# A Fourier layer and a soft mixture of experts on one core: the head's loads, warm-up matmuls and first units in another order

## The chip, the core and the metric

The kernel runs as one launch on one core of a Trainium2 chip. The metric is the device time of a run in microseconds (us), taken as the median over several runs. A core has five engines, each with its own queue that is worked strictly in order: TensorE (PE in the profile, with its weight loads as PEld), VectorE (DVE), ScalarE (ACT), GpSimd (POOL) and SyncE (SP). SP issues nearly all DMAs here, ACT the few that the head's first stores and, after the change, one load need.

## The reference, cut to what matters

```python
X = np.fft.rfft(x, axis=1)                       # x: 8 x 2496 x 256, float32
Yr = Xr @ w_r - Xi @ w_i + b_r
Yi = Xr @ w_i + Xi @ w_r + b_i
Y = softshrink(Yr, 0.01) + 1j * softshrink(Yi, 0.01)
y = np.fft.irfft(Y, n=2496, axis=1).reshape(19968, 256)
logits = y @ phi                                 # 32 slots: 8 experts x 4
d = softmax(logits over all 19968 tokens)        # dispatch
slot_out = per expert: relu(d.T @ y @ w1) @ w2
out = softmax(logits over the 32 slots) @ slot_out
```

## The kernel before, in words

The transform of length 2496 = 39 x 64 is done as two small ones. **Stage a** (`a_unit`, L326) multiplies 117 rows of x (three sets of 39) by the constant `f1a`, two columns of 64 at a time: a *unit*, 512 wide, whose result `pa` lies in PSUM. A batch has 11 units. ACT or DVE copies each `pa` into a staging tile `ast`, and `ast` is stored to DRAM (`adr`, or `ad0` for the first 48 rows of batch 0), because the second transform needs the data with other rows on the partitions. **Stage b** runs in steps of four of the 20 frequencies: `load_ap` (L384) reads a group back as `ap` in two DMAs, `f2` (L392) multiplies it by `smov` into `px` (two halves c = 0, 1), ACT and DVE split `px` into a high and a low part (`xth`, `xtl`) and do the same with the sum of its real and imaginary parts (`xsm`, split into `xsh`, `xsl`). `lin_k` (L445) and `lin_y` (L456) multiply these by the split weights into `pk` and `py`; DVE adds bias and shrinks (`ut`, `rt`, whose last subtraction is POOL's). Later stages project on phi (`pq`), transpose (`pt`), and run the inverse transform and the softmaxes on 32 slots for each batch, then the experts, then the output.

Batch 0 is special: its x comes as eleven loads (`x0`), all units are plain fp32 (`direct`: one matmul instruction in the program, which the profile shows as two), and its stores are cut in two. The rows that groups 0 and 1 need go to `ad0` by four stores on ACT's queue; the other 80 rows wait in the list `rest` and are stored by SP later. Batch 1 begins inside the head as well: its first four units are fp32 too (`nd` is 4), and their two staging tiles are kept in `held` until SP's list calls for their store. From the fifth unit on the rows are split into `xh` (ACT) and `xl` (POOL), and a unit is three matmuls.

The order of all engines is written by hand. Each piece of work is a generator that yields the time at which it wants to go on (in units of the plan, not in us); a heap (`run_until`) replays them in that order, and `keep_in_program_order` freezes it. The numbers of the dictionary `PLAN` (L118 on) are these wishes: `a1` for the units of batch 1, `kw` for the warm-up matmuls (`keep_warm`, products of a zero tile that nobody reads), `seq` for the order of SP's DMAs in the head (`a0` is `load_ap` of group 0, `r` the next of the four rest stores, `w4` and `w0` the held stores, `x8` a load of batch 1's x, `c` and `k` constants, `s` the second part of `smov`). Tiles come from pools with few buffers: `ap` has 3, `ast` 3, `wr` 3, `xr` 3; a tile that takes a used buffer waits for its last reader.

DMAs report on eight semaphores in turn (DMAHW0 to DMAHW7), in the order in which the program issues them, SP's and ACT's together. A DMA waits until the previous one on its semaphore has landed, so the ninth waits for the first.

Of the kernel before, what the change touches and what calls it, by code (L numbers as in the profile page):

```python
# [11 lines left out]
F32 = mybir.dt.float32  # L12
F32R = mybir.dt.float32r
AF = mybir.ActivationFunctionType
ALU = mybir.AluOpType
AX = mybir.AxisListType

B, N, D = 8, 2496, 256
# [32 lines left out]
def _constants():  # L51
# [95 lines left out]
    "f1": [1.5, 2.15],  # L147
    "kw": [[-40, 9]],
    "ap1": 1.85,
# [8 lines left out]
    "cl_": 'V',  # L158
    "a1": [-50, -49, -48, -47, 3.0, 4.0, 5.9, 6.9, 7.9, 8.9, 10.2],
    "e1": [0, 0, 0, 0, 0, 0, 0, 0, 1, 0, 1],  # L160
# [4 lines left out]
    "lsl": 'PPPPPPPPPPPPPPPPPPPPPPPV',  # L165
    "ast4": {(0, 18): "wr", (1, 0): "wr", (1, 4): "ap"},
    "nd": 4,
    "x1": {(1, 20): 3.5, (2, 0): 7.2},
    "ab1": [[0, 4], [4, 8], [8, 14], [14, 20], [20, 22]],
    "seq": ['a0', 'c', 'a1', 's', 'x8', 'r', 'r', 'r', 'r', 'w4', 'a2', 'x9', 'x10', 'w0', 'k'],  # L170
}
# [12 lines left out]
def fourier_soft_moe_kernel(ctx: ExitStack, tc: tile.TileContext, t: dict, out: bass.AP):  # L184
# [51 lines left out]
    def sp(**kw):  # L236
        tc.keep_in_program_order(nc.sync.dma_start(**kw))
# [16 lines left out]

    def load_x(i):
        if i >= len(xorder) or xorder[i] in xrs:
            return
        b, g = xorder[i]
        ng = min(xc, G - g)
        xr = wtile([PX, xc, D], F32, "xr", f"xr{b}_{g}")  # L260
        sp(out=xr[:, :ng, :], in_=x[b, :, g : g + ng, :])
        xrs[(b, g)] = xr
# [63 lines left out]
    def a_unit(b, g, u):  # L326
# [26 lines left out]
        ast = asts[(b, gs[0])]  # L353
        po = psum(("pf", "pl", "pt")[i_ % 3] if first else "pf", f"pa{b}_{g}")
        if direct:
            mm(out=po, lhsT=f1a, rhs=xs, start=True, stop=True)
        else:
            mm(out=po, lhsT=f1h, rhs=xh, start=True, stop=False)
            mm(out=po, lhsT=f1h, rhs=xl, start=False, stop=False)
            mm(out=po, lhsT=f1l, rhs=xh, start=False, stop=True)  # L360
        yield tu + PLAN['ao']
        copy(
# [4 lines left out]
        if g + GP == gs[1]:  # L367
            if b == 1 and direct:
                held[gs[0]] = (ad[b], ast, *gs)
                return  # L370
            yield tu + 1.0
            if first:
                a_write(ad0, ast, *gs, 0, R * 4 * KG, q=aq)
                rest.append((ad[b], ast, *gs, R * 4 * KG, QA))
            else:
                a_write(ad[b], ast, *gs)
# [7 lines left out]
    def load_ap(b, grp):  # L384
        ap = wtile([128, KG, D], F32, "ap", f"ap{b}_{grp}")
        src = (ad0 if b == 0 and grp < 2 else ad[b]).rearrange("(k r) g d -> k (r g) d", r=R)
        src = src[grp * 2 * KG : (grp + 1) * 2 * KG, :N2]
        for c in range(2):
            sp(out=ap[c::2], in_=src[c * KG : (c + 1) * KG].rearrange("k n d -> n k d"))
        return ap  # L390

    def f2(s, c, t0):  # L392
        yield t0
        b, grp = steps[s]
        ap = aps[s]
        ps = psum("pf", f"px{b}_{grp}_{c}")
        for j in range(KG):
            k = grp * KG + j
            q = k if grp == 0 else k - KG
            rhs = smov[min(grp, 1)][:, 0 : q + 2 : q + 1, :]  # L400
            mm(
                out=ps[:, j * 128 : (j + 1) * 128],
                lhsT=ap[:, j, c * 128 : (c + 1) * 128],
                rhs=rhs,
                start=True,
                stop=True,
            )
        yield t0 + PLAN['xho']
        xh = wtile([128, 2, KG, 64], F32R, "xth", f"xth{b}_{grp}_{c}")
        xl = wtile([128, 2, KG, 64], F32R, "xtl", f"xtl{b}_{grp}_{c}")  # L410
        pv = ps.rearrange("p (j c q) -> p c j q", j=KG, c=2)
        sm = wtile([128, KG, 64], F32, "xsm", f"xsm{b}_{grp}_{c}")
        sh = wtile([128, KG, 64], F32R, "xsh", f"xsh{b}_{grp}_{c}")
        sl = wtile([128, KG, 64], F32R, "xsl", f"xsl{b}_{grp}_{c}")
        A.copy(out=xh, in_=pv)
        A.copy(out=sm, in_=pv[:, 0])
        yield t0 + PLAN['xlo']
        V.tensor_tensor(out=xl, in0=pv, in1=xh.bitcast(F32), op=ALU.subtract)
        V.tensor_tensor(out=sm, in0=pv[:, 1], in1=sm, op=ALU.add)
        yield t0 + PLAN["sho"]  # L420
        copy(E_("sh"), sh, sm)
        yield t0 + PLAN["slo"]
        (L_("sl", s, c) if s else V).tensor_tensor(out=sl, in0=sm, in1=sh.bitcast(F32), op=ALU.subtract)
        xts[(s, c)] = (xh, xl, sh, sl)

# [19 lines left out]
    def lin_k(s):  # L445
        t0 = 4 * s
        yield t0 + 0.35
        b, g = steps[s]
        pk = psum("pl", f"pk{b}_{g}")
        for c in range(2):  # L450
            lin_s(pk, c, xts[(s, c)])
        yield t0 + PLAN['ko']
        kss[s] = wtile([128, 2, 256], F32, "k1", f"k1{b}_{g}")
        A.copy(out=kss[s], in_=pk.rearrange("p (e x) -> p e x", e=2))

    def lin_y(s, e):  # L456
        b, grp = steps[s]
        end = s == ns - 1
        t0 = 4 * s + 1 + (PLAN["T_"]["ye"] if end else 1.35) * e
        yield t0  # L460
        py = psum("pl", f"py{b}_{grp}_{e}")
        lin(py, e, 0, xts[(s, 0)])
        if e == 1 and not end:
            t0 = 4 * s + 3
            yield t0
# [300 lines left out]
    sp(out=wri, in_=t["w"])  # L766
    load_x(7)
    for u, g in enumerate(range(0, G, GP)):
# [494 lines left out]
```

## Time and profile before

| | us |
|---|---|
| median of 3 runs | 567.42 |
| lowest and highest of them | 566.44 and 567.63 |
| the profiled execution | 563.34 |
| its span, first to last instruction | 561.5 |
| PE busy in the span | 521.4 |
| first product of group 0 (`px`) starts at | 23.53 |
| first product of group 2 starts at | 39.68 |

The profile is of one execution. The timeline lists an engine's instructions in order of time: start, length, engine, line, operation, out<-in, count, and in brackets how long the engine had stood idle and what ended that. The windows view gives, for chosen stretches, each engine's busy time, the clock that the PE was granted (1.00 is full), the busy share of the 16 DMA engines and the rate of their traffic. The chain of waits is followed back from the end: at each step to what released the instruction. An engine's idle time matters only where that engine, or what it feeds, is what the rest waits for. All helpers record their instructions under one line (L243 for matmuls, L180 for the other engines, L237 and L240 for DMAs on SP and ACT), so the tiles' names tell the pieces apart.

### The profile page before, as it was taken

How to read it: one execution, taken by the hardware profiler on the slowest of the kernel's cores; microseconds unless marked ns; L12 is line 12 of the kernel's file. 1: busy time of each engine (PE TensorE's matmuls, PEld its weight loads, DVE VectorE, ACT ScalarE, POOL GpSimd, SP SyncE). 2: the span in 40 equal slices, each digit the busy share in tenths (PEclk: the TensorE clock that was granted, in tenths of full speed). 3: DMA queues.
4: the chain of work that ended last, by engine and by line, in shares of the span. 5: the costliest groups of instructions: out<-in, count | busy, mean ns of one | idle time of the engine just before them, and what ended most of it. 6: DMA issues, size and time to landing. Idle time of an engine off the chain costs nothing.

```text
span 561.5 us, 11780 instructions
## 1 busy us (share of the span) xinstructions
PE 521.4 (93%) x4354; PEld 442.2 (79%) x4354; DVE 422.0 (75%) x837; ACT 298.1 (53%) x650; POOL 281.1 (50%) x258
## 2 busy tenths in 40 slices
PE   8669999999999999999999999999899979899794
PEld 4458999989898889889988898987687867367573
DVE  0347897799979897989789978986795764248783
ACT  4435555666566656665665666653433333147572
POOL 0037777766766576658655866684554402000100
PEclk9999999999999999999999999999999998999899
DMA  8788464756476637664757474766634378979898
GB/s 301 249 294 292 151 207 152 210 179 170 163 216 207 189 118 208 207 180 167 204 171 199 155 201 167 222 230 178 186 131 126 113 183 276 392 240 368 325 374 351
DMA packets 93684, 121.44 MB, mean 216 GB/s; under 512 B 46786, under 2 KB 68736, under 8 KB 93628
## 3 DMA queue, kind: packets, MB, share of 16 engines
q1 hardware_dynamic: 93372, 119.63, 65.4%
q10 hardware_dynamic: 256, 1.08, 0.5%
q8 instruction: 34, 0.56, 0.4%
q14 instruction: 22, 0.18, 0.1%
HBM read 69.87 MB, written 50.82 MB: 215 GB/s over the span
## 4 chain that ended last, share of the span: by engine, by line
PE 70%; DVE 13%; DMA 10%; ACT 3%; issue 2%; SPq 1%; ACTq 0%; DVEq 0%
PE py L243 16%; PE px L243 11%; PE pq L243 9%; PE pa L243 8%; PE pk L243 7%; PE pt L532 4%; PE pr L243 3%; DMA eb<-ed 2%; PE pc L1067 2%; DMA ad<-ast 2%; PE pe L243 2%; DMA ap<-adr 2%; DVE mx L180 1%; DVE clpL L180 1%; DVE xtl L180 1%
## 5 line engine op out<-in xcount | busy, mean ns | idle before, releaser
L180 POOL TENSOR_TENSOR rt<-ut,rt 128x512 f32<-128x512 f32 x79 | 111.7, 1414 | 24.4 <-DVE rt L180 18.4
L180 POOL TENSOR_TENSOR xsl<-xsm,xsh 128x256 fp32r<-128x256 f32 x77 | 59.3, 770 | 102.4 <-DVE xsh L180 71.0
L180 POOL TENSOR_TENSOR xl<-xr,xh 117x512 fp32r<-117x512 f32 x73 | 98.5, 1350 | 22.6 <-ACT xh L180 14.7
L243 PE MATMUL px<-smov,ap 128*128 128x128 f32 x640 | 85.6, 277 | 8.0 <-DMA ap<-adr 4.5
L243 PEld LDWEIGHTS px<-smov,ap 128*128 128x128 f32 x640 | 80.3, 193 | 13.7 <-issue 8.1
L180 ACT CAST xth<-px 128x512 fp32r<-128x512 f32 x80 | 46.8, 585 | 73.0 <-PE py L243 37.6
L180 ACT COPY ast<-pa 128x512 f32<-128x512 f32 x86 | 50.3, 587 | 64.5 <-PE pa L243 61.6
L180 DVE SCALAR_TENSOR_TENSOR ut<-py,pk,k 128x256 f32<-128x256 f32 x160 | 69.5, 475 | 15.0 <-PE py L243 13.1
L180 DVE TENSOR_TENSOR xtl<-px,xth 128x512 fp32r<-128x512 f32 x80 | 54.6, 682 | 26.8 <-ACT xsm L180 22.0
L243 PE MATMUL py<-xth,nwsh 128*128 128x256 f32 x160 | 53.5, 334 | 0.0
L180 DVE TENSOR_SCALAR rt<-ut 128x512 f32<-128x512 f32 x69 | 52.2, 756 | 0.5
L243 PE MATMUL pk<-xsh,w_rh 128*128 128x256 f32 x160 | 47.9, 300 | 2.0 <-DVE xsh L180 2.0
L180 ACT COPY T<-pt 128x512 f32<-128x512 f32 x70 | 42.1, 601 | 9.0 <-PE pt L532 7.3
L532 PE MATMUL pt<-pk,rt 128*128 128x128 f32 x320 | 45.9, 273 | 0.9 <-DVE dd L180 0.6
L243 PE MATMUL pk<-xsl,w_rh 128*128 128x256 f32 x160 | 45.1, 282 | 0.0
L243 PE MATMUL pk<-xsh,w_rl 128*128 128x256 f32 x160 | 44.9, 281 | 0.0
L243 PE MATMUL py<-xtl,nwsh 128*128 128x256 f32 x160 | 44.7, 279 | 0.0
L243 PE MATMUL py<-xtl,wdh 128*128 128x256 f32 x160 | 44.7, 279 | 0.0
L243 PE MATMUL py<-xth,wdl 128*128 128x256 f32 x160 | 44.7, 279 | 0.0
L243 PE MATMUL py<-xth,nwsl 128*128 128x256 f32 x160 | 44.7, 279 | 0.0
L243 PE MATMUL py<-xth,wdh 128*128 128x256 f32 x160 | 44.7, 279 | 0.0
L243 PE MATMUL pq<-rhs,ct 128*128 128x512 f32 x156 | 43.1, 415 | 0.3 <-DVE ost L180 0.3
(186 smaller groups left out, 1241.7 us busy)
## 6 DMA issues: line engine op xcount, KB each, us to landing
ap<-adr SPq DMA_DIRECT2D x76, 256.0 KB
out<-ost SPq DMA_DIRECT2D x37, 512.0 KB
xr<-in_x SPq DMA_DIRECT2D x35, 512.0 KB
adr<-ast SPq DMA_DIRECT2D x20, 768.0 KB
w<-in_moe_w SPq DMA_DIRECT2D x25, 512.0 KB
adr<-ast SPq DMA_DIRECT2D x8, 512.0 KB
w<-in_moe_w SPq DMA_DIRECT2D x14, 256.0 KB
x<-in_x SPq DMA_DIRECT2D x11, 256.0 KB
```

The source lines that it names most:

```text
L180: return lambda *a, **k: self.tc.keep_in_program_order(f(*a, **k))
L243: tc.keep_in_program_order(nc.tensor.matmul(**kw))
L532: tc.keep_in_program_order(nc.tensor.transpose(out=out, in_=in_, identity=identity))
L1067: nc.tensor.transpose(out=pc[:, i * P1 : (i + 1) * P1], in_=chls[b][x][:, 2 * (r + i) : 2 * (r + i) + 2].rearrange("p g h s -> p (g h s)") ...
```

## The change

It touches only the head. The load of the second piece of batch 1's x (`xr1_4`, 512 KB) leaves SP's queue, where it stood ahead of the loads of group 0, and is issued by ACT behind the last of the four `ad0` stores. The two units that need it move behind the first `px`, on two other PSUM buffers (`pt` in place of `pf`). The run of warm-up matmuls grows from 9 to 18. SP's order is changed, and with it two buffers: `ap0_0` and `ap0_1` get theirs first, and the staging tile of those two units is one of the three `ast` buffers, no longer an `ap` one. For the first step DVE forms the sum `xsm` and its split before the split of `px` itself, and PE takes `pk` and `py` half by half. From group 2's product on, each engine's order is the same as before, but for the store of that staging tile, which SP now issues later.

```diff
-    "kw": [[-40, 9]],
+    "kw": [[-40, 18]],
...
-    "a1": [-50, -49, -48, -47, 3.0, 4.0, 5.9, 6.9, 7.9, 8.9, 10.2],
+    "a1": [-50, -49, -1.7, 0.42, 3.0, 4.0, 5.9, 6.9, 7.9, 8.9, 10.2],
...
-    "ast4": {(0, 18): "wr", (1, 0): "wr", (1, 4): "ap"},
+    "ast4": {(0, 18): "wr", (1, 0): "wr"},
     "nd": 4,
+    "nh": 2,
+    "ao1": {2: 1.2, 3: 0.2},
...
-    "seq": ['a0', 'c', 'a1', 's', 'x8', 'r', 'r', 'r', 'r', 'w4', 'a2', 'x9', 'x10', 'w0', 'k'],
+    "seq": ['a0', 'r', 'a1', 'c', 's', 'r', 'x8', 'r', 'r', 'a2', 'x9', 'x10', 'w0', 'k'],
...
-    def load_x(i):
+    def load_x(i, q=None):
...
-        sp(out=xr[:, :ng, :], in_=x[b, :, g : g + ng, :])
+        (q or sp)(out=xr[:, :ng, :], in_=x[b, :, g : g + ng, :])
...
-        po = psum(("pf", "pl", "pt")[i_ % 3] if first else "pf", f"pa{b}_{g}")
+        po = psum(("pf", "pl", "pt")[i_ % 3] if first else "pt" if b == 1 and i_ in PLAN["ao1"] else "pf", f"pa{b}_{g}")
...
-            if b == 1 and direct:
+            if b == 1 and i_ < PLAN["nh"]:
                 held[gs[0]] = (ad[b], ast, *gs)
                 return
             yield tu + 1.0
             if first:
                 a_write(ad0, ast, *gs, 0, R * 4 * KG, q=aq)
                 rest.append((ad[b], ast, *gs, R * 4 * KG, QA))
+                if gs[1] == G:
+                    load_x(7, aq)
...
-        ap = wtile([128, KG, D], F32, "ap", f"ap{b}_{grp}")
+        ap = ap_early.pop(0) if ap_early else wtile([128, KG, D], F32, "ap", f"ap{b}_{grp}")
...
-        V.tensor_tensor(out=xl, in0=pv, in1=xh.bitcast(F32), op=ALU.subtract)
+        if s:
+            V.tensor_tensor(out=xl, in0=pv, in1=xh.bitcast(F32), op=ALU.subtract)
...
+        if not s:
+            V.tensor_tensor(out=xl, in0=pv, in1=xh.bitcast(F32), op=ALU.subtract)
...
         for c in range(2):
             lin_s(pk, c, xts[(s, c)])
+            if s == 0 and c == 0:
+                yield t0 + 0.45
...
-    load_x(7)
+    ap_early = [wtile([128, KG, D], F32, "ap", f"ap0_{grp}") for grp in range(2)]
```

SP's queue from the first weights to the load of group 2, before. Here `xr1_8` is the third piece of batch 1's x, `adr0` are the rest stores of batch 0, `pk0` is a packed constant with the biases and phi:

```order
L237 DMA wri_111<-in_w 128x1024
L237 DMA xr1_4_134<-in_x 128x1024
L237 DMA ap0_0_194<-ad0_129 64x4x256 x2
L237 DMA pk0_112<-in_pk0 128x216
L237 DMA ap0_1_198<-ad0_129 64x4x256 x2
L237 DMA smov1_110<-in_smov 128x1088
L237 DMA xr1_8_202<-in_x 128x1024
L237 DMA adr0_136<-ast0_0_137 80x1536
L237 DMA adr0_136<-ast0_6_147 80x1536
L237 DMA adr0_136<-ast0_12_158 80x1536
L237 DMA adr0_136<-ast0_18_169 80x1024
L237 DMA adr1_178<-ast1_4_186 128x1024
```

The same stretch now:

```order
L239 DMA wri_111<-in_w 128x1024
L239 DMA ap0_0_134<-ad0_129 64x4x256 x2
L239 DMA adr0_136<-ast0_0_137 80x1536
L239 DMA ap0_1_135<-ad0_129 64x4x256 x2
L239 DMA pk0_112<-in_pk0 128x216
L239 DMA smov1_110<-in_smov 128x1088
L239 DMA adr0_136<-ast0_6_147 80x1536
L239 DMA xr1_8_197<-in_x 128x1024
L239 DMA adr0_136<-ast0_12_158 80x1536
L239 DMA adr0_136<-ast0_18_169 80x1024
```

In both the loads of group 2 come next. Between the loads of group 0 and those of group 2 the same transfers stand as before, two of the rest stores now ahead of `xr1_8`, one of them ahead of group 1; gone are `xr1_4` (ahead of group 0) and the store of `ast1_4`, which now stands behind the constant `pk1`, after the loads of group 2.

ACT's queue from the third `ad0` store on, before, with what each instruction waits for:

```order
L240 DMA ad0_129<-ast0_12_158 48x1536 [waits DMAHW2_49,Activation_49]
L180 COPY ast0_18_169<-pa0_18_170 128x512 [waits PE_49]
L180 COPY ast0_18_169<-pa0_20_174 128x512 [waits PE_49]
L240 DMA ad0_129<-ast0_18_169 48x1024 [waits DMAHW3_49,Activation_49]
L180 COPY ast1_0_179<-pa1_0_180 128x512 [waits PE_49]
L180 COPY ast1_0_179<-pa1_2_183 128x512 [waits PE_49]
L180 COPY ast1_4_186<-pa1_4_187 128x512 [waits PE_49]
```

And now:

```order
L242 DMA ad0_129<-ast0_12_158 48x1536 [waits DMAHW1_49,Activation_49]
L182 COPY ast0_18_169<-pa0_18_170 128x512 [waits PE_49]
L182 COPY ast0_18_169<-pa0_20_174 128x512 [waits PE_49]
L242 DMA ad0_129<-ast0_18_169 48x1024 [waits DMAHW2_49,Activation_49]
L242 DMA xr1_4_178<-in_x 128x1024 [waits DMAHW3_49]
L182 COPY ast1_0_181<-pa1_0_182 128x512 [waits PE_49]
```

With one DMA fewer ahead of them the stores have moved by one semaphore: DMAHW2 is the first `ad0` store's, on which the third store waited and now the fourth does.

PE's queue from the last unit ahead of the warm-up run to the first `py`, before:

```order
L243 MATMUL pa1_2_183<-xr1_0_130,f1a_81 128x512
L243 MATMUL pa1_4_187<-xr1_4_134,f1a_81 128x512
L243 MATMUL pa1_6_190<-xr1_4_134,f1a_81 128x512
L243 MATMUL wps532_218<-warm_72 128x512 x9
L243 MATMUL px0_0_0_242<-smov0_109,ap0_0_194 128x128 x4
L243 MATMUL px0_0_1_247<-smov0_109,ap0_0_194 128x128 x4
L243 MATMUL pk0_0_274<-xsh0_0_0_255,w_rh_228 128x256
```

And now:

```order
L245 MATMUL pa1_2_185<-xr1_0_130,f1a_81 128x512
L245 MATMUL wps527_210<-warm_72 128x512 x18
L245 MATMUL px0_0_0_243<-smov0_109,ap0_0_134 128x128 x4
L245 MATMUL px0_0_1_248<-smov0_109,ap0_0_134 128x128 x4
L245 MATMUL pa1_4_254<-xr1_4_178,f1a_81 128x512
L245 MATMUL pk0_0_279<-xsh0_0_0_259,w_rh_229 128x256
```

The unit `pa1_4` now stands behind the `px` of group 0; its twin `pa1_6` follows the first half of `pk` and `py`, before the second half.

More of the change, by code (lines that the diff above doesn't have):

```diff
@@ L360, in a_unit @@
             mm(out=po, lhsT=f1l, rhs=xh, start=False, stop=True)
-        yield tu + PLAN['ao']
+        yield tu + (PLAN["ao1"].get(i_, PLAN["ao"]) if b == 1 else PLAN["ao"])
         copy(
@@ L459, in lin_y @@
         t0 = 4 * s + 1 + (PLAN["T_"]["ye"] if end else 1.35) * e
-        yield t0
+        if s == 0 and e == 0:
+            yield t0 - 0.6
+        else:
+            yield t0
         py = psum("pl", f"py{b}_{grp}_{e}")
         lin(py, e, 0, xts[(s, 0)])
+        if s == 0 and e == 0:
+            yield t0
         if e == 1 and not end:
```

## The prediction

> **What bounds the kernel now.** I read the page first, then the chain of waits of the head, then the timelines of PE, SP and ACT there, and last the windows view for DMA traffic and clock.
>
> ```profile
> PE 521.4 (93%) x4354; PEld 442.2 (79%) x4354; DVE 422.0 (75%) x837; ACT 298.1 (53%) x650; POOL 281.1 (50%) x258
> 70.00:120.00 50.00, 49.18 (x436) 45.56 (x436) 42.23 (x82) 29.92 (x65) 35.66 (x31) 1.00 0.58 183
> ```
>
> PE is busy 98% of the stretch from 70 to 120 us (49.18 of 50): the body is bound by PE, so a time saved before it is a time saved at the end. The head is another matter. The chain of waits there, start and length:
>
> ```profile
> 8.60 5.60 DMA ad<-ast
> ...
> 15.74 3.19 DMA ad<-ast
> ...
> 35.53 4.01 DMA ap<-adr
> ```
>
> The fourth `ad0` store lands at 15.74 + 3.19 = 18.93 and only then SP issues the load of group 0. The second link ends at 39.54 with the load of group 2, which PE awaits. PE's side, with the idle time ahead of each piece:
>
> ```profile
> 4.38 10.44 PE L243 MATMUL pa<-x,f1a 117*128 117x512 f32 x22
> 14.65 1.88 PE L243 MATMUL pa<-xr,f1a 117*128 117x512 f32 x4
> 17.84 1.96 PE L243 MATMUL pa<-xr,f1a 117*128 117x512 f32 x4 [1.30 <-DMA xr<-in_x]
> 19.23 2.63 PE L243 MATMUL wps<-warm 128*128 128x512 f32 x9
> 23.53 2.02 PE L243 MATMUL px<-smov,ap 128*128 128x128 f32 x16 [1.67 <-DMA pk<-in_pk]
> ...
> 31.16 1.95 PE L243 MATMUL px<-smov,ap 128*128 128x128 f32 x16
> ...
> 39.68 1.72 PE L243 MATMUL px<-smov,ap 128*128 128x128 f32 x8 [3.71 <-DMA ap<-adr]
> ...
> 52.45 1.06 PE L243 MATMUL px<-smov,ap 128*128 128x128 f32 x8
> ```
>
> The widest hole is 3.71 us ahead of group 2. Whatever PE saves earlier only widens it; the end moves with the time at which group 2 lands. SP's queue says what sets that:
>
> ```profile
> 18.98 1.34 SPq L237 DMA_DIRECT2D ap<-ad x2
> ...
> 34.89 1.62 SPq L237 DMA_DIRECT2D ap<-adr x2
> ```
>
> From the issue of group 0's load to that of group 2's pass 34.89 - 18.98 = 15.91 us, in which SP has the DMA engines move group 0, group 1, `smov`, `xr1_8` and the four rest stores. The traffic in three stretches (last columns: clock, DMA share, GB/s):
>
> ```profile
> 14.00:17.00 3.00, 2.53 (x6) 0.75 (x4) 0.46 (x2) 1.99 (x4) 0.00 (x0) 1.00 1.02 418
> 18.60:20.10 1.50, 1.50 (x5) 0.76 (x4) 0.39 (x1) 0.85 (x2) 0.00 (x0) 1.00 0.00 0
> 28.00:31.00 3.00, 2.48 (x19) 2.13 (x18) 1.05 (x3) 1.03 (x2) 0.00 (x0) 1.00 1.04 420
> ```
>
> The DMA engines are full before 17, empty from 18.6 to 20.1 (the stores have landed, the load's first data have not come), and full again later. The load that the change moves, 512 KB or 0.52 MB, stands now in the full stretch ahead of the last stores, and would stand in the empty one.
>
> **The change part by part.** *The load of `xr1_4` behind the stores.* Ahead of the fourth store the DMA engines have 0.52 MB less to move: 0.52 / 0.418 = 1.25 us. The other bound is the issue on ACT:
>
> ```profile
> 13.14 0.58 ACT L180 COPY ast<-pa 128x512 f32<-128x512 f32 x1 [0.27 <-PE pa L243]
> 14.28 0.31 ACTq L240 DMA_DIRECT2D ad<-ast x1
> 14.63 1.08 ACT L180 COPY ast<-pa 128x512 f32<-128x512 f32 x2 [0.91 <-DMA ad<-ast]
> 15.74 0.31 ACTq L240 DMA_DIRECT2D ad<-ast x1
> ```
>
> The third store stood waiting for the first to land (8.60 + 5.60 = 14.20, the same semaphore); with one DMA fewer ahead it waits for a load long landed and goes when its copy ends, 13.14 + 0.58 = 13.72, about half a us earlier. The last copy can't start before PE ends batch 0 (4.38 + 10.44 = 14.82) and takes 0.58, so the fourth store is issued at about 15.45 instead of 15.74; it now waits for the first store, landed at 14.20. If it took its own 3.19 us again it would land at 18.64, a gain of only 0.29. The shortest way of a DMA in these rows is that of `f1a`, issued at 0.74:
>
> ```profile
> 2.59 0.23 DVE L180 CAST f1h<-f1a 117x128 fp32r<-117x128 f32 x1 [1.20 <-DMA f1a<-in_f1a]
> ```
>
> 1.85 us, for 64 KB: with that the store lands at 17.30, a gain of 1.6. So the gain lies between 0.29 and 1.6; I take 1.25, the traffic's, since the 3.19 us were spent in a queue that is 1.25 us shorter. The load itself costs ACT 0.31 us of issue, ahead of copies that nobody waits for, and 1.25 us of DMA time. I cost it at nothing, because 18.60:20.10 is empty; without that cover it costs up to 1.25 us at group 0 and all that follows.
>
> *Eighteen warm-up matmuls.* They start when the first four `pa` matmuls of batch 1 end, 14.65 + 1.88 = 16.53. At 2.63 / 9 = 0.29 each they take 5.3 and end at 21.8. The first `px` is due at 23.53 - 1.25 = 22.28: half a us to spare, so nothing; even a gain of 1.6 us (21.9) would not meet them.
>
> *The two units behind `px`.* Their 1.96 us of PE work go between 23.53 and 31.16, where PE now stands idle for 1.44 and 0.52 us:
>
> ```profile
> 26.99 0.39 PE L243 MATMUL pk<-xsh,w_rh 128*128 128x256 f32 x1 [1.44 <-DVE xsh L180]
> 28.71 0.39 PE L243 MATMUL pk<-xsh,w_rh 128*128 128x256 f32 x1 [0.52 <-DVE xsh L180]
> ```
>
> DVE's new order lets `pk` start one subtraction earlier. All this is covered by the 3.71 us hole, so it counts nothing; uncovered it would be 1.96 at most.
>
> *SP's new order.* The stretch from group 0 to group 2 carries the same bytes, so I keep its 15.91 us and let group 2 be issued 1.25 us earlier, at 33.64; it lands at about 38.3 and the first product starts at 38.43. Inside the stretch some come later: two rest stores (0.49 MB each) now stand ahead of `xr1_8`, so it lands 2 x 0.49 / 0.420 - 1.25 = 1.1 us later than now. It had landed by the time ACT read it:
>
> ```profile
> 30.56 0.62 ACT L180 CAST xh<-xr 117x512 fp32r<-117x512 f32 x1
> ```
>
> so by 31.65 at the latest. That is a new wait: behind this cast on ACT stand the copies of group 1's `px`, and PE, DVE and POOL behind them. PE is then ready for group 2 at about 36, as now (39.68 - 3.71 = 35.97), and 2.4 us of the hole remain as cover. Two further waits are new. ACT's copy of `pa1_4` takes over the first staging buffer and needs that rest store landed, which SP issues right behind group 0 at about 19.1; ACT gets there only behind its copies of the first `px`, which ends at 23.53 + 2.02 - 1.25 = 24.3. And the held-back `ast1_4` store now delays group 3's load by 0.52 / 0.418 = 1.25 us, which eats the lead of that load; PE reaches group 3 only at 52.45 and found it there without waiting, so nothing.
>
> *Behind the gate.* Two things could hold the 1.25 us back or add to it: the clock, and POOL.
>
> ```profile
> 36.64:40.05 3.41, 0.37 (x3) 0.40 (x4) 0.87 (x3) 0.00 (x0) 1.95 (x2) 1.00 0.86 255
> 40.05:43.46 3.41, 3.41 (x15) 3.12 (x15) 0.00 (x0) 1.37 (x3) 1.27 (x1) 0.50 1.00 328
> 401.86:405.28 3.42, 1.75 (x30) 1.25 (x22) 1.71 (x4) 0.93 (x3) 1.70 (x3) 1.00 0.88 190
> 405.28:408.69 3.41, 2.70 (x20) 2.44 (x21) 3.23 (x7) 1.36 (x5) 0.87 (x1) 1.00 0.83 289
> 521.33:524.74 3.41, 1.53 (x10) 1.01 (x9) 3.25 (x5) 1.74 (x4) 1.37 (x1) 1.00 0.99 396
> 524.74:528.15 3.41, 3.41 (x13) 2.82 (x12) 2.17 (x4) 1.19 (x3) 0.00 (x0) 0.50 0.62 245
> ```
>
> After a stretch of 3.41 us in which PE was busy for 0.37 or 1.53 us the clock is halved for the next 3.41 us; after one with 1.75 it is not. So 1.66 us idle are allowed and 1.88 are not. The new hole of 2.4 us crosses that in most positions of the stretch against it: (2.4 + 3.41 - 2 x 1.77) / 3.41 = two thirds. I therefore leave the halved clock in, and the head's lead stays 1.25 us. Where it does not fall, PE wins 3.41 / 2 = 1.7 us more, but POOL then binds:
>
> ```profile
> 45.19 0.23 DVE L180 CAST sinvh<-pk 128x128 fp32r<-128x128 f32 x1 [7.68 <-DMA pk<-in_pk]
> 49.55 2.55 POOL L180 TENSOR_TENSOR xl<-xr,xh 117x512 fp32r<-117x512 f32 x2
> 51.17 0.43 PE L243 MATMUL pa<-xh,f1h 117*128 117x512 f32 x1
> ```
>
> DVE starts again when the constant `pk1` lands at 45.19, POOL works on from there, and the first of its two subtractions at 49.55 ends at about 50.83, 0.34 us before PE uses it at 51.17. `pk1` stands in SP's queue behind group 2 and moves with it. So the lead can grow to 1.25 + 0.34 = 1.6 us, and to 1.25 + 1.7 = 2.95 only if POOL's spans are worth less than they look.
>
> The page "TensorE: Matmul & The Clock Gate" of the Trainium skill (Part 1, on what is actually happening) has the clock fall only after at least one idle window of about 3.4 us, in windows that run free of the kernel's start. By that rule a hole of 2.4 us would keep the full clock, and the sum would be 1.6 us. The row at 521.33 speaks against it, since PE was busy 1.53 us of that stretch and the clock fell; that the phase is free no single run shows.
>
> The sum: -1.25 for the store, 0 for the rest. In the profiled execution's terms 563.34 - 1.25 = 562.1. The median of the runs, 567.42, lies 4.08 above that execution; the head's waits are the same work in both, so I take the 1.25 off the median: 566.2.
>
> **The rivals.** *The clock stays up.* For it: the hole shrinks from 3.71 to 2.4. Against: the two thirds above. It gives 567.42 - 1.6 = 565.8, at the very best 564.5.
>
> *The lead is lost.* The fourth store is bound by its own latency, gains 0.29, and all behind follows: 567.1. For it: the store's row shows 3.19 us while the DMA engines were emptying already; writes put between the 1 KB reads of groups 0 and 1 could eat some of the lead as well. Against: 418 GB/s right up to 17.
>
> *`xr1_4` gets in group 0's way, slower.* If the stores gain only 0.29, the load, issued at about 15.8 behind them, still moves when group 0 is asked for. At the slowest rate in the rows above with busy DMA engines, 255 GB/s at 36.64, it takes 0.52 / 0.255 = 2.0 us; group 0 and with it group 2 come up to 2.0 - 0.29 = 1.7 us later, 569.1. It decides, against no change, from the point at which the load holds group 0 up by more than the stores have gained. Against: 1.5 us empty at 18.6. The page "DMA: Bandwidth & Descriptors" (queues, rings and completion order) has each DMA engine take turns between the queues, a packet of one and then of the other, so ACT's queue would give group 0 no precedence; no row here shows the two queues apart.
>
> **How the numbers follow.** Forecast 0.50, clock stays up 0.16, lead lost 0.25, in the way 0.09. A measurement tells about 0.2% from no change (the three runs span 566.44 to 567.63), 1.13 us: faster means below 566.29. The forecast's own range, 565.6 to 566.8 (the store's gain 0.6 to 1.8), crosses that line, and I give 0.36 of its 0.50 to faster and 0.14 to same. Faster: 0.36 + 0.16 = 0.52. Same: 0.14 + 0.25 = 0.39. Slower: 0.09. The range reaches down to the best of the clock case, 564.5, and up over the lost lead, to 567.6; it leaves out the slower case.
>
> **What would show it.** The load of group 0 issued at about 17.7 in SP's timeline, the first `px` at 22.3 with an idle time under 1.7; no hole at `xr1_4`; ACT waiting at its first cast of `xr1_8` until about 31.6; group 2 issued at about 33.6 and its first product at 38.4, after an idle time of 2.4; DVE's `sinvh` at about 43.9; the clock's row behind the gate at 0.50. It is wrong if group 0 comes early and group 2 does not (SP's order costs the lead), if the empty DMA stretch is still there and the load stands elsewhere, or if PE's hole moves to another place.

## The result, and the profile after

The changed kernel takes 572.25 us (median of 5 runs, 566.44 to 574.67) where the kernel before took 567.42 in the same session: a ratio of 1.0105, 95% interval 1.0063 to 1.0148. It is slower by 3.6 to 8.4 us. Two later measurements, on two chips, gave 1.0067 (1.0035 to 1.0099) and 1.0085 (1.0053 to 1.0117). The prediction had 566.2 and a range of 564.5 to 567.6. The ratios leave out runs that lie more than 1.5% above the fastest of their kernel, while medians and ranges are of all runs.

The profiled execution of the changed kernel took 574.67 us; that of before took 563.34. From its page, the span, TensorE, and the queue that fetches TensorE's program (packets, MB, share of the DMA engines):

```profile
span 572.9 us, 11800 instructions
PE 529.0 (92%) x4363; PEld 447.9 (78%) x4363; DVE 424.3 (74%) x837; ACT 297.8 (52%) x650; POOL 281.3 (49%) x258
q8 instruction: 35, 0.57, 0.4%
```

The page of before has 34 packets in the last of these rows:

```profile
q8 instruction: 34, 0.56, 0.4%
```

0.57 MB in 35 packets is 16 KB each. The prediction passed over this row, which turned out to matter most.

The head after, on PE (start, length, and in brackets the idle time ahead):

```profile
15.95 4.67 PE L245 MATMUL wps<-warm 128*128 128x512 f32 x18
23.21 3.55 PE L245 MATMUL px<-smov,ap 128*128 128x128 f32 x16 [2.58 <-DMA adr<-ast]
...
31.14 1.95 PE L245 MATMUL px<-smov,ap 128*128 128x128 f32 x16
...
39.97 1.96 PE L245 MATMUL px<-smov,ap 128*128 128x128 f32 x8 [2.98 <-DMA ap<-adr]
```

And the issues on SP, and the moved load on ACT:

```profile
18.22 1.40 SPq L239 DMA_DIRECT2D ap<-ad  x2
...
20.30 2.92 SPq L239 DMA_DIRECT2D ap<-ad  x2
...
35.50 1.25 SPq L239 DMA_DIRECT2D ap<-adr  x2
```

```profile
15.80 0.49 ACTq L242 DMA_DIRECT2D xr<-in_x  x1
```

The windows view, with PE's busy time first and the clock, DMA share and GB/s last:

```profile
18.60:20.10 1.50, 1.50 (x8) 1.23 (x8) 0.18 (x1) 0.17 (x1) 1.25 (x1) 1.00 0.55 191
19.58:22.99 3.41, 1.05 (x5) 0.54 (x3) 0.00 (x0) 0.00 (x0) 0.58 (x1) 1.00 0.84 254
22.99:26.40 3.41, 3.19 (x15) 3.23 (x16) 0.22 (x1) 0.86 (x2) 0.00 (x0) 0.50 0.91 245
```

The stretch that was empty of traffic is filled (0.55, was 0.00), group 0's load goes out 0.76 us earlier (18.22, was 18.98), and the first product starts 0.32 earlier (23.21, was 23.53). But the hole ahead of it grew to 2.58 us, the clock was halved behind it, and group 2's product came 0.29 us later than before. That is a third of a microsecond. Two more are lost just behind it, where the load `xr1_12` lands at 44.61 (41.25 in before); in the chain of waits, start and length:

```profile
36.84 7.77 DMA xr<-in_x
```

But the two traces are 11.4 us apart, and most of that opens late: the same TensorE instruction, the 1400th matmul from the end, starts at 366.28 in before and at 368.62 after (2.3 us), so 9 us are lost behind it, where the change moves nothing.

TensorE in the tail, before and then after; `pd` is the product that waits for `eb`, a small read that comes back from DRAM in 128-byte pieces:

```profile
478.39 1.31 PE L243 MATMUL pd<-eb,pk 128*128 128x320 f32 x4 [1.13 <-DMA eb<-ed]
```

```profile
486.97 2.25 PE L245 MATMUL pd<-eb,pk 128*128 128x320 f32 x4 [3.41 <-DMA eb<-ed]
```

The same wait is three times as long. One trace of each could not say whether that was the change or the day: in 35 runs of one session before alone spans 560.88 to 570.23.

### The profile page after: what moved, and what is told of

The parts are those of the page before. It is cut to its first block, busy times and chain, and to the rows that moved or that the text cites. A ratio compares the mean times of both kernels' runs of the same rounds, so it can differ in the third digit from the quotient of the medians.

```text
span 572.9 us, 11800 instructions
## 1 busy us (share of the span) xinstructions
PE 529.0 (92%) x4363; PEld 447.9 (78%) x4363; DVE 424.3 (74%) x837; ACT 297.8 (52%) x650; POOL 281.3 (49%) x258
## 4 chain that ended last, share of the span: by engine, by line
PE 71%; DVE 14%; DMA 7%; ACT 3%; issue 3%; SPq 1%; POOL 0%; ACTq 0%; DVEq 0%
PE py L245 15%; PE px L245 10%; PE pa L245 9%; PE pq L245 9%; PE pk L245 7%; PE pt L546 4%; PE pr L245 3%; PE pc L1081 2%; DMA eb<-ed 2%; DVE mx L182 2%; PE pe L245 2%; DVE clpL L182 1%; DVE xtl L182 1%; DVE clpd L182 1%; DMA gp<-gd 1%
## 5 line engine op out<-in xcount | busy, mean ns | idle before, releaser
L245 PE MATMUL px<-smov,ap 128*128 128x128 f32 x640 | 88.2, 283 | 7.9 <-DMA ap<-adr 3.0
L245 PEld LDWEIGHTS px<-smov,ap 128*128 128x128 f32 x640 | 82.9, 198 | 13.4 <-issue 7.3
```

What stands on the lines that cost most here:

```text
L245: tc.keep_in_program_order(nc.tensor.matmul(**kw))
```

## The experiments

**Is it the change, and which part?** Four kernels on one chip, 32 runs of before beside them (median 565.87).

*The changed kernel again,* no edit.

> The changed kernel as it is, once more, beside the kernel before on another chip or day. Theory A (the change itself costs, by a later head and by where the body then meets the clock's windows): 570 to 574 us again, 3 to 7 us over before, with the first px at half clock from about 23.0 us (a hole of 2.4 to 2.7 us ahead of it) and the load xr1_12 landing at 43.5 us or later (41.25 in before). Theory B (the extra 5 us was this chip's memory in these runs, many slow packets): the median comes out within 1.5 us of before, and the tail's gaps shrink to the sizes of before (2.81 us ahead of the last group's writes, 1.13 us ahead of eb).

571.0 us, ratio 1.0067 (1.0035 to 1.0099). It belongs to the change. Yet in this trace the first product had the full clock and the tail's holes were nearly those of before, so neither half of theory A or B fits as it was put. The trace is of the fastest of the twelve runs, 567.02 us.

*Thirty dummies.*

```diff
-    "kw": [[-40, 18]],
+    "kw": [[-40, 30]],
```

> The changed kernel with 30 dummies of 0.26 us in place of 18, so that TensorE is busy until about 23.7 us and the first px follows with next to no hole. Theory A1 (the half clock at 23.0 to 26.4 us, in which px took 3.55 us instead of 2.02, is what loses the lead): the clock stays up there, group 1's px comes 1 us or more earlier than 31.14, group 2's px 0.5 to 1.3 us earlier than 39.97, and the time falls by 1 to 3 us against the changed kernel. Theory A2 (group 2 waits for SyncE's queue and the transfers, as the prediction had it for this term): the clock stays up but group 2's px stays within 0.3 us of 39.97 and the time stays within 1 us of the changed kernel, but for what the later windows make of it.

567.39 us, 1.0031 (1.0002 to 1.0059): 3.6 us under the changed kernel. The bridge itself did what it should, the hole ahead of `px` is gone and the clock stays up:

```profile
15.61 7.39 PE L245 MATMUL wps<-warm 128*128 128x512 f32 x30
22.84 1.95 PE L245 MATMUL px<-smov,ap 128*128 128x128 f32 x16
...
39.12 2.05 PE L245 MATMUL px<-smov,ap 128*128 128x128 f32 x8 [2.20 <-DMA ap<-adr]
```

By its own words that was a win for A1, the half clock in the head, though 3.6 us is more than the 1 to 3 that A1 gave. It was the wrong reading, as the cut kernels below show.

*Before, with the body pushed back.*

```diff
-'du': [[-4.5, 0],
+'du': [[-156.0, 11], [-4.5, 0],
```

> The kernel before, its head untouched, with 11 fp32 dummies of 128x128 on TensorE (about 2.3 us at the granted rate) at about 70 us, which only push the rest of the body later. Theory C (a shift of the body against the fixed 3.41 us windows of the clock is what brings the extra half-speed stretches at 408, 487 and 535 us): the time rises by more than the 2.3 us put in, by 4 to 8 us, with stretches of half clock in new places after 400 us. Theory D (the windows are not decisive, the extra came from the transfers of those runs): the time rises by 1.5 to 3 us, and the half-clock stretches stay those of before, each moved by at most one window.

569.39 us, 1.0060 (1.0034 to 1.0086), 3.5 us over before for 2.3 us put in. That lies between the two theories and decides nothing yet; the table below adds 1.2 us at the end to the 2.3. Its trace, whose head is that of before, has `xr1_12` landing at 44.05: a late landing there needs no change.

*SyncE's old order in the changed kernel* (`ast4` as in before, and `seq` but for its `w4`).

> The changed kernel with SyncE's old order (c ahead of a1, four r's behind x8) and the wait of the stores of batch 1's first group put back, the rest of the change kept. Theory A3 (the stores pulled ahead on SyncE make the reads of group 1 and of xr1_12 late): adr0_18 lands at 34.8 us instead of 35.36, xr1_12 at 41 to 42 instead of 44.6, VectorE's wait for pk falls from 9.45 us to 7 or less, and the time falls by 2 to 3 us against the changed kernel. Theory A4 (the order is not it; the piece xr1_4 behind the last store and the half clock at 23 us are): xr1_12 still lands at 43.5 or later and the time stays within 1 us of the changed kernel.

570.75 us, 1.0075 (1.0043 to 1.0108), while `xr1_12` landed at 43.27, between the two theories. SyncE's order is not the loss.

**Where is it?** Kernels that end early show the loss up to a place. The rest of the program is left out and a filler is stored, so only their times against each other count:

```diff
-    run_until(TB - 0.02)
+    run_until(20)
+    eps = psum("ps", "end")
+    mm(out=eps, lhsT=warm[:, 0:128], rhs=warm, start=True, stop=True)
+    eo = wtile([128, F], F32, "wr", "eo")
+    for h in range(2):
+        A.copy(out=eo[:, h * 512 : h * 512 + 512], in_=eps)
+    for j in range(2):
+        sp(out=out[j], in_=eo)
```

> The kernel before, cut off behind the work of planner time 20 (about 65 us, two groups behind group 2): everything later is left out, and two stores of a filler follow TensorE's last matmul, so the time is that of the head alone. About 70 us. It is the base for the three cut kernels beside it; its spread over the runs shows how much the head alone varies. The profiled runs of before and of the shifted kernel, which have the same head, differed by 1.9 us at 59 us, so a spread of 2 us or more is expected.

92.5 us (91.8 to 93.65, 5 runs).

> The changed kernel cut off at the same place. Theory H (the whole loss of the change arises in the head): the mean is 3 to 5 us over that of the cut kernel before, as the whole kernels differ by 3.8. Theory T (the head loses little on average and the rest arises where the later body meets the windows of the clock, or in the tail): 0 to 1.5 us over.

91.47 us (90.75 to 92.73, 7 runs): a microsecond *less* by the medians.

> The changed kernel with 30 dummies, cut off at the same place. Theory H1 (the hole of 2.5 us ahead of the first px makes a part of the loss through the half clock behind it): 1.5 to 3.5 us below the cut changed kernel, as the whole kernels differ by 3.4 on average. Theory H2 (that hole costs nothing in the head, since group 2 waits for the transfers): within 0.7 us of it.

92.13 us (91.11 to 93.5, 6 runs).

> The changed kernel with 30 dummies, SyncE's old order and the old wait of the stores of batch 1's first group, cut off at the same place: what is left of the change is the second piece of batch 1's x behind the last store, the units put off, and VectorE's order. If SyncE's order carries a loss of its own (the stall of 1.8 to 2.3 us on the second read of group 1, xr1_8 behind two more stores), it lies 1 us or more below the cut kernel with 30 dummies alone, and at the level of the cut kernel before or under it; if not, within 0.7 us of it.

92.39 us (90.54 to 92.84, 6 runs). As shares of the time of the whole kernel before, the four are 0.1629, 0.1616, 0.1620 and 0.1608, so the first changed head is some 0.7 us the shorter. The planner times were misjudged: TensorE's last matmul ends at 82 to 84 us in the first two traces. Up to there the changed head loses nothing, nor do 30 dummies gain anything over 18. Theory T. Next, the cut at planner time 130 and the whole kernels on one chip:

> The changed kernel a third time, beside its own cut versions on one chip, so that the loss of the whole kernel and that of its first 330 us are measured together. If the loss belongs to the change: 2 to 6 us over before, as in the two measurements so far (5.9 and 3.8 us). If it belongs to one chip or one hour: within 1.5 us of before.

571.53 us, 1.0085 (1.0053 to 1.0117).

> The kernel before, cut off behind the work of planner time 130 (about 330 us; the stretch from 385 us on, with its holes, is left out, two stores of a filler end it). Base for the cut kernel beside it. Head and body without the tail: the spread should be that of the head alone, some 2 us, and smaller than the 8 us of the whole kernel if the tail adds its own.

392.8 us (392.62 to 393.97, 4 runs).

> The changed kernel cut off at the same place. Theory H (the loss is in place before the tail, whatever the cut at 80 us showed): 3 to 5 us over the cut kernel before. Theory T (head and body lose nothing on average, the loss arises behind 380 us, in the windows of the clock and the transfers of the tail): within 1 us of it, while the whole kernel beside it is slower by 3 us or more.

393.25 us (392.47 to 393.91, 5 runs): 0.45 over, where the whole kernel is 6.0 over by the medians. This cut too fell later than planned: TensorE's last matmul ends at 382 us in one trace and 383 in the other. The loss arises in the last third. There every engine has the same instructions in the same order in both, but for those that handle semaphores.

> The changed kernel with 30 dummies, on a second chip. If the bridge to the first px is what decides, it lies 2 to 4 us below the changed kernel again and 0 to 2.5 us over before; if the difference of the first measurement (3.4 us) was that chip's, it lies within 1.5 us of the changed kernel.

567.74 us, 1.0038 (1.0014 to 1.0062): 3.8 us under the changed kernel on a second chip. So twelve dummies at 16 to 23 us change the whole time, though at the first cut they change next to nothing. A shift in time is an unlikely reason, for before and after were still within half a microsecond of each other at the second cut. What dummies do change for good is the length of TensorE's program ahead of the tail.

**The program's place in its blocks.** TensorE's instructions come in packets of 16 KB on queue q8. Counting TensorE's recorded instructions (matmuls, weight loads and those that handle semaphores) between two fetches gives 255 on the mean, and the places, counted from the end, hang on how long the program is: with nine more matmuls (18 instructions) a fetch stands at 1019 to 1031 instructions from the end, just ahead of `pd` (1011 to 1004), and a 35th one at 3 or 4 from the end; in before the fetch comes behind `pd` (922) and there is no 35th. A test crosses the two heads with three lengths. Tiny matmuls behind the dummies lengthen the program without changing the order of anything else:

```diff
-    "kw": [[-40, 9]],
+    "kw": [[-40, 9, 9]],
...
-    def keep_warm(t, n):
+    def keep_warm(t, n, m):
...
+        for _ in range(m):
+            mm(out=ps[:, 0:16], lhsT=warm[:, 0:128], rhs=warm[:, 0:16], start=True, stop=True)
```

> The kernel before with nine tiny matmuls (16 columns) behind its nine dummies, in the hole of 1.67 us ahead of the first px: no wait and no order changes, but TensorE's program is longer by nine matmuls, as the changed kernel's is, so that everything behind lies at other places of its 16 KB blocks of instructions. Theory P (the fetch of one of these blocks, which falls 1.6 to 1.8 us behind the issue of the read of eb in the changed kernel and makes that read 5.5 to 6.1 us long instead of 3.9, makes most of the loss): 568.5 to 571 us, 3 to 5 us over before, with the hole ahead of pd at 477 us at 2.5 us or more. Theory Q (the loss comes with the changed head, by its transfers or by its shift): within 1 us of before.

570.33 us, 1.0077 (1.0043 to 1.0110): **before, with nine tiny matmuls added, is as slow as the changed kernel.** In its trace they did move the first product, from 23.53 to 25.15, but not that of group 2, which starts at 39.62 (39.68 in before) with 2.04 us of the hole left:

```profile
20.75 4.54 PE L243 MATMUL wps<-warm 128*128 128x512 f32 x18
25.15 2.03 PE L243 MATMUL px<-smov,ap 128*128 128x128 f32 x16
...
39.62 1.78 PE L243 MATMUL px<-smov,ap 128*128 128x128 f32 x8 [2.04 <-DMA ap<-adr]
```

> The same with 21 tiny matmuls: the place in the blocks is that of the changed kernel with 30 dummies, which was 1.1 and 2.2 us over before; so theory P gives 1 to 2.5 us over before, and the fetch less than 0.5 us behind the issue of the read of eb. Theory Q: within 1 us of before.

569.23 us, 1.0060 (1.0028 to 1.0093). That is 3.4 us by the ratio, more than the 1 to 2.5 expected. The 21 tiny ones took 2.4 us and moved the first product, but TensorE still waited 2.1 us ahead of group 2, so the head doesn't explain the rest; it stays open.

*The changed kernel with nine dummies,* `"kw": [[-40, 9]]`:

> The changed kernel with the nine dummies of before: the place in the blocks is that of before, and the hole ahead of the first px grows to some 4.8 us. Theory P: the time falls by 3 us or more against the changed kernel, to within 1.5 us of before, in spite of the longer hole. Theory Q: it stays 3 us or more over before, and the longer hole can only add to it.

564.48 us, 0.9992 (0.9965 to 1.0019): **the changed kernel without its nine extra matmuls is back at before,** with a hole of 4.68 us ahead of the first product and the half clock behind it:

```profile
23.17 3.40 PE L245 MATMUL px<-smov,ap 128*128 128x128 f32 x16 [4.68 <-DMA adr<-ast]
```

*The changed kernel with 18 dummies and 12 tiny ones,* `"kw": [[-40, 18, 12]]`:

> The changed kernel with twelve tiny matmuls behind its 18 dummies: the place in the blocks is that of the kernel with 30 dummies, while the hole ahead of the first px stays over 1.5 us. Theory P: 1 to 2.5 us over before, like the kernel with 30 dummies, 2 to 4 us below the changed kernel. Theory Q (the bridge over the hole is what the 30 dummies brought): at the level of the changed kernel, 4 to 5 us over before.

568.42 us, 1.0055 (1.0028 to 1.0082). Like 30 dummies, or a little above, with a hole of 1.26 us left. That is 3.1 us by the ratio where P gave 1 to 2.5. So theory P's numbers hold in the two tests with nine or none, and with 21 more the loss is 0.6 to 0.9 us above its range. Q holds in none.

How a fetch does it is seen in the read of `eb`. SP's issue of its two halves, before and with nine tiny matmuls:

```profile
473.96 1.34 SPq L237 DMA_DIRECT2D eb<-ed  x2
```

```profile
478.34 1.34 SPq L237 DMA_DIRECT2D eb<-ed  x2
```

What the DMA queues carry from there until `pd` starts, before (473.9 to 478.4) and with nine (478.2 to 484.8):

```profile
DMA packets 2753, 0.92 MB, mean 205 GB/s; under 512 B 2608, under 2 KB 2608, under 8 KB 2753
...
q1 hardware_dynamic: 2753, 0.92, 90.6%
```

```profile
DMA packets 2843, 1.24 MB, mean 188 GB/s; under 512 B 2623, under 2 KB 2623, under 8 KB 2842
...
q1 hardware_dynamic: 2842, 1.22, 77.9%
q8 instruction: 1, 0.02, 1.0%
```

One packet of instructions, and the rest is the same small pieces. A DMA is spread over 16 engines, and the trace has a signal from each. The landing of the 16 parts of `eb`'s second half, in us from the issue of the first:

```
before                 3.90 3.91 3.98 ... 4.21 4.23 4.24 4.29
nine tiny matmuls      3.81 3.81 3.82 ... 4.31 4.57 4.58 6.37
changed kernel         3.89 3.90 3.93 ... 4.39 4.53 4.55 6.56
```

Fifteen parts have landed by 4.6 us and one comes 1.8 to 2.0 us behind them, and `pd` waits for the last part. The trace doesn't name the DMA engine of a packet, so that the late part's engine is the one that fetched the 16 KB is inferred. What speaks for it: in all six traces with a fetch 2.0 to 2.7 us behind the issue the last part lands at 4.72 to 6.56, always one alone, and in the three without a fetch in the read at 4.29 to 4.65. How late it is differs, from 0.4 us (the changed kernel's second trace) to 2.2. Then the clock adds to it:

```profile
484.84 2.47 PE L243 MATMUL pd<-eb,pk 128*128 128x320 f32 x4 [3.22 <-DMA eb<-ed]
```

```profile
480.24:483.65 3.41, 1.38 (x13) 1.14 (x11) 1.75 (x3) 1.17 (x2) 1.40 (x4) 1.00 0.99 221
483.65:487.06 3.41, 2.22 (x4) 1.17 (x4) 0.49 (x1) 0.19 (x1) 0.00 (x0) 0.50 0.86 305
487.06:490.47 3.41, 3.41 (x27) 1.49 (x26) 0.49 (x1) 0.10 (x1) 0.00 (x0) 0.50 1.02 411
```

PE was busy 1.38 us in the first stretch, and the clock was halved for the next two. The second place is the end of the kernel. GB/s in 40 slices from 2 us ahead of TensorE's last matmul to the end, before and with nine, then what SP waits for there:

```profile
GB/s 393 377 426 426 410 393 377 410 377 442 377 426 426 377 442 360 443 377 426 360 442 377 410 459 360 442 344 361 401 377 393 385 189 25 0 0 0 0 0 0
```

```profile
GB/s 334 392 420 377 391 435 406 333 435 348 406 377 435 420 377 406 391 449 420 363 420 421 420 348 377 399 377 391 290 51 29 29 22 29 7 0 0 0 0 0
```

```profile
SPq L1259 <- DMA out<-ost: 2.9, 1, 2.9
```

```profile
SPq L1261 <- DMA out<-ost: 4.0, 1, 4.0
```

The 22 to 29 GB/s behind the full rate are a sixteenth of it: one engine, with 1.2 us of stores left. In each of the last three stores one part of the 16 lands 1.1 to 1.4 us behind the other 15 in all ten traces with a fetch within 5 us of the end of TensorE's work, and at most 0.4 us behind them in the four without.

The trace splits the loss so. The tail runs from the 1400th matmul from the end to the end; a fetch is given in us behind the issue of `eb`; the last column counts halved stretches of 3.41 us between 380 us and TensorE's end:

```
more matmuls   kernel               tail    fetch   eb to pd   last matmul to end   halved
   0           before              195.2    none      4.42          7.97             2
   0           after, 9 dummies    196.1    none      4.50          7.99             2
   0           the same, again     196.2    none      4.78          8.00             2
  +3           before + 3 tiny     195.6    2.37      5.37          8.00             2
  +9           after               204.3    2.41      6.69          9.27             5
  +9           after, again        196.0    2.02      4.86          9.23             1
  +9           after, third time   203.4    2.20      6.55          9.33             5
  +9           after, old order    201.7    2.29      6.15          9.35             4
  +9           before + 9 tiny     202.3    2.66      6.50          9.25             5
 +21           after, 30 dummies   195.5    1.04      5.13          9.04             1
 +21           the same, again     199.4    0.84      5.06          9.10             2
 +21           after + 12 tiny     198.7    0.56      4.73          9.23             3
 +21           before + 21 tiny    197.6    0.76      4.70          9.14             2
 +22           before, shifted     196.3    0.69      4.87          9.15             2
```

With nine more the tail takes 201.5 us on the mean of five, 5.7 over the 195.8 of the three without: 1.3 at the end, 1.6 in the read of `eb`, and a rest of 2.8 that goes with two more halved stretches (up to 3.41 / 2 = 1.7 each). A halved stretch at 483 to 487 us stands in the four traces in which `eb` took over 6 us and in no other: 6 stretches in the five traces. The other halved stretches lie elsewhere, and that they follow from the fetch is not shown. With 21 more the fetch comes within 1.1 us of the issue and costs the read 0.1 to 0.6; the end costs 1.1 to 1.2.

*The two terms apart, and the rest of the change once more:*

```diff
-    "kw": [[-40, 9]],
+    "kw": [[-40, 9, 3]],
```

> The kernel before with three tiny matmuls in the hole ahead of the first px. By the places of the fetches in the traces (1023 to 1027 TensorE instructions from the end with nine more matmuls, 18 instructions; pd stands at 1012 to 1005 from the end) the block's fetch would come at about 1014, in the last matmuls ahead of pd, so still inside the read of eb; the 35th block, which is fetched 3 instructions from the end with nine more, is not reached with three more. Theory P with two terms apart: the hole ahead of pd is 2.5 us or more, as with nine, but the stretch from TensorE's last matmul to the end stays at 7.97 us instead of 9.2; so 2 to 3.5 us over before, some 1.2 us under the kernel with nine. If a little of the lengthening does nothing and only the 35th block costs: within 0.7 us of before.

568.36 us, 1.0030 (0.9998 to 1.0062). The stretch behind the last matmul stays at 8.00, as expected, and the fetch falls 2.37 us behind the issue. But the hole is 2.05, less than the 2.5 expected, and the interval just reaches no change: the split holds for the end, and for the read only in direction.

```profile
482.11 1.31 PE L243 MATMUL pd<-eb,pk 128*128 128x320 f32 x4 [2.05 <-DMA eb<-ed]
```

> The changed kernel with nine dummies once more, to settle whether what is left of the change gains anything when TensorE's program keeps its places in the blocks: by the first measurement 0.4 us under before (ratio 0.9992, 0.9965 to 1.0019), and by the medians 0.9 us. If the rest of the change is worth something, 0.5 to 1.5 us under before again; if not, within 0.5 us of it.

566.58 us beside 566.03 for before, ratio 0.9996 (0.9968 to 1.0024). With its program at the old length the rest of the change can't be told from nothing, and no version here beats before by more than that.

## Why the prediction was wrong, step by step

*The step that failed* is "Eighteen warm-up matmuls ... half a us to spare, so nothing". It priced them by the time that they take on PE and found the hole that covers it. Their price was elsewhere: 18 more TensorE instructions push all that follows along its 16 KB blocks, one block's fetch falls into the read of `eb` 460 us later, a 35th falls into the last stores, and the hole that the first makes halves the clock. The term put at nothing measured 4.4 us by the ratio: adding nine tiny matmuls to before costs 1.0077, and taking nine dummies from the changed kernel gives 0.9992. That the lengthened program is the cause is shown both ways. The way from there is shown for the late part of `eb` and of the last stores; that the rest of the loss is the clock's is argued from the halved stretches. The prediction's last section said that it would be wrong "if PE's hole moves to another place"; it did, but the prediction had looked for one in the head only. No rival had the mechanism. The slower rival, `xr1_4` in group 0's way, did not happen: in 13 traces with the changed head group 0's first product starts at 23.2 on the mean, not later than the 23.53 of before. (Its price was misread too: it took 255 GB/s for the slowest rate with busy DMA engines, but the row at 401.86 has 190 at a share of 0.88.)

*The sum's one term, 1.25 us by the earlier store,* was right in kind and too large where it counts. Means over 7 traces with the old head and 13 with the new, the cut kernels among them:

```
                               old head   new head   earlier by
load of group 0 issued           19.46      18.43      1.03
load of group 2 issued           35.70      35.00      0.70
first product of group 2         40.40      39.67      0.73
200 matmuls behind group 2       67.86      67.43      0.43 (standard errors 0.45 and 0.30)
```

The load of group 0 gained 1.03 of the 1.25. The stretch from group 0 to group 2, which the prediction kept at 15.91 us, is 16.2 in the old head and 16.6 in the new. What reaches the body is 0.4 on the mean with an error as large; the cut kernels have some 0.7 us less at 82 us and 0.45 more at 382. The gain is not shown in any time, but neither is it refuted.

*The load `xr1_4` at nothing:* the empty stretch took it (DMA share 0.55 at 18.60:20.10), as the prediction put it, but not all: 191 GB/s for 1.5 us are at most 0.29 of its 0.52 MB, and part of the rest moves beside the load of group 0.

*The dummies' length:* 5.3 us were expected, 4.67 measured, and they started at 15.95 rather than 16.53. So they ended at 20.63, the hole was 2.58 where half a microsecond was expected, and the clock fell ahead of the first product in that trace. With 30 the hole goes, and the time of the cut head does not fall (92.13 against 91.47): the prediction's cover, the hole ahead of group 2, held.

*SP's order:* restoring it changes nothing (570.75 against 571.0).

*The clock behind the gate* stayed halved, as forecast (0.43 us busy in the stretch ahead). The forecast's rule from two rows fits the tail as well, where a hole of 3.2 us ahead of `pd` was followed by half clock, but its limit is not sharp, as the counts at the end show.

*The base* was one lucky trace: with 195.2 us its tail is the shortest of fourteen, and its head is the earliest of its kind (65.69 at 200 matmuls behind group 2, where the mean of seven is 67.86).

## What to carry to other kernels

Dummy instructions need not be free when they hide in a hole: they lengthen their engine's program, and everything behind lies elsewhere in its 16 KB blocks. When a change adds or takes instructions and a far, untouched part gets slower, look at the `instruction` queue in the DMA view there, and at whether one of a transfer's 16 parts lands late. The test costs one run: add as many tiny instructions to the old kernel, or take as many from the new. And where one kernel's runs spread over 9 us, cut kernels off at two or three places before believing a difference of two traces.

## What the runs showed of the hardware

- With a fetch of 16 KB of program (its packet takes 0.9 to 1.2 us) beside a transfer that is spread over all 16 engines, one part of the 16 landed late: by 0.4 to 2.2 us in the read of `eb`, by 1.1 to 1.4 in the last stores. Both are transfers whose end is waited for. Up to the cut at 382 us the 24 fetches cost nothing that the times show (393.25 against 392.8 with the places shifted). The Trainium skill, page "Runtime: NRT & Kernel Launch", section on instruction fetch mechanics, has programs streamed in blocks of 16 KiB, 256 instructions, fetched ahead at a cost that is mostly hidden. The traces agree on the block (0.57 MB in 35 packets, 255 recorded instructions on the mean); the cost was 1.3 us at the end and 1.6 on the mean at `eb`, so at these two places it was not hidden.
- The clock: in the 20 traces, of the stretches of 3.41 us that lie between the first full clock and TensorE's last matmul, all 38 at full clock with PE busy under 1.5 us were followed by half clock, 20 of 28 with 1.5 to 1.7, 6 of 34 with 1.7 to 2.1, and 1 of 2384 above. The page "TensorE: Matmul & The Clock Gate" of the Trainium skill (Part 1, what's actually happening) asks for an idle window of about 3.4 us; these rows ask for little more than half of one. Its free-running windows agree with the traces: the first edge lies 0.08 to 2.51 us behind a kernel's start, different from trace to trace. That the two first traces had it nearly alike (2.50 and 2.51) was chance. By the phase the same hole can cost up to 3.41 / 2 = 1.7 us or nothing, an estimate: a hole of 2.58 us was followed by half clock in the first trace of the changed kernel, one of 2.43 us in the second by full clock.
- The issue of group 1's two reads, behind three transfers on SP, held its queue for 2.92 us in the changed trace, where that of group 0 took 1.40. With SP's old order, in which that issue took 1.24, the time stayed (570.75 us against 571.0).
